# Attention and two MLPs on one core: last rows' scores from block-diagonal queries, the low parts of the first MLP's input made per chunk on VectorE, and a new order

## The chip, the cores and the metric

The kernel runs on one core of a Trainium2 chip. TensorE (PE in the profile) multiplies matrices, VectorE (DVE), ScalarE (ACT) and GpSimd (POOL) do the work between, and SyncE (SP) issues the transfers; each engine takes its own instructions in order. PEld are the loads of the matmuls' stationary operands. The metric is the device time of one launch in microseconds (us).

## The reference, cut to what matters

```python
def _attn_ref(q, k, v, tau):                      # 4 x 8 heads, 576 rows, 64 wide
    scores = (1.0 / np.sqrt(q.shape[-1])) * np.matmul(q, k.transpose(0, 1, 3, 2))
    thresh = np.max(scores, axis=-1, keepdims=True) - tau
    scores = np.where(scores >= thresh, scores, -1000000000.0)
    attn = np.exp(scores - np.max(scores, axis=-1, keepdims=True))
    attn = attn / (np.sum(attn, axis=-1, keepdims=True) + 1e-09)
    return np.matmul(attn, v)
...
x = attn_out, heads side by side                  # 2304 tokens x 512
h = x @ w_in                                      # 512 -> 2048
x = (h * np.tanh(softplus(h))) @ w_out            # first MLP, 2048 -> 512
g = x @ w_gate                                    # 512 -> 1536
x = (g * sigmoid(g) * (x @ w_val)) @ w_out2       # second MLP, 1536 -> 512
```

The weights of the MLPs come as 64-bit words and are turned into floats on the chip.

## The kernel before, in words

**Precision.** A 32-bit factor is split into a high part (the value cast to fp32r, a 32-bit format of TensorE) and a low part (the value less its high part). A product is three matmuls: high with high, high with low, low with high.

**Attention.** Two heads form a pair, and the 16 pairs run one after the other, overlapped. For pairs after the first, `load` brings q and k (128 partitions: 64 dimensions of each head), POOL scales q (L216), ACT casts the high part (L219), POOL makes the low part (L222), and `stack` copies the pieces by 12 transfers into `stk`, where the 128 partitions hold the high part of one head above its low part, so that one matmul covers two of the products. A head has 576 rows: four blocks of 128 and a rest of 64. So a pair has nine score tiles `s`: eight full ones (four matmuls each, 576 columns in two pieces of 320 and 256, each twice), and tile 8, which holds the last 64 rows of both heads. Tile 8 is made by `scores` at L89 with ten matmuls, from columns where the two heads' last rows stand side by side: first all 128 rows against the second head's keys, then the first 64 rows again against the first head's keys. Per tile, DVE takes the row maximum (`rowmax`, L108), POOL adds the threshold (`thresh`, L112), ACT takes the exponential (L118), DVE masks and sums (`mask`, L126). PE transposes the masked rows (L149), ACT copies them to `pt` (L155 to L162), and `av` (L172, 20 matmuls for each of two halves) multiplies by the values. Three score tiles fit in PSUM at once (`s=3`), so a tile waits for the mask of the one three before it.

**First MLP.** Tokens are taken in chunks of 512, the last has 256. For a group of columns of `w_in`, each chunk has a unit per column block: `project` (L533, 12 matmuls, here called a U), the activation on ACT (L565), a high part `gh` on ACT (L550), a low part `gl` on DVE (L553), and `down` (L544, 12 matmuls, here called a D). The chunks' inputs are split too: `x_hi` on ACT (L557) and `x_lo` (L560), the latter on POOL for the chunks after the first, as soon as attention has ended. Chunk 0's parts `x0h` and `x0l` are made during attention. Weights are turned into floats by DVE steps (L445 to L466, `cg` and `cn`), one integer addition on POOL (L452), a cast on ACT (L471) and a low part on DVE (L476); four tiles named `early` are done during attention.

**Order.** All operations of a stage are entered in a planner (`Plan`) with an engine, a cost, what they come after, what slots they take and free, and a rank. For attention the ranks alone fix each engine's order (tables `RANK`, `EARLY`, `XEARLY`); for the MLPs the planner takes, of the operations that are ready, the one with the lowest rank (`MRANK`).

Of the kernel before, what the change touches and what calls it, by code (L numbers as in the profile page):

```python
# [9 lines left out]
F32 = mybir.dt.float32  # L10
# [6 lines left out]
P = 128  # L17
# [27 lines left out]
def attention(tc, cst, q, k, v, x, beside=None, S=576):  # L45
# [18 lines left out]
    ps = ctx.enter_context(tc.tile_pool(name="a_ps", bufs=2, space=PSUM))  # L64

    def load(p, nm, h=None):
        src = dict(q=q, k=k, v=v)[nm][p]
        if nm == "v":
            t = pw.tile([P, 10, 64], F32, tag="vn", name=f"vn{p}", bufs=SLOTS["vn"])
        elif h is None:  # L70
            t = pl.tile([P, S], F32, tag="n", name=f"{nm}n{p}", bufs=SLOTS["n"])
        else:
            if nm + "n" not in st[p]:
                st[p][nm + "n"] = pw.tile([P, 1152], F32, tag="pp", name=f"{nm}d{p}", bufs=SLOTS["pp"])
            for r in (0, 64):
                nc.sync.dma_start(out=st[p][nm + "n"][r:r + 64, S * h:S * h + S], in_=src[64 * h:64 * h + 64, :])
            return
        nc.sync.dma_start(out=t, in_=src)
        st[p][nm + "n"] = t


    def scores(p, i):
# [129 lines left out]
    def inputs(p, nm, what, eng=None):  # L212
# [4 lines left out]
        elif what == "hi":  # L217
            d[nm + "h"] = pl.tile([P, S], F32R, tag="hh", name=f"{nm}h{p}", bufs=SLOTS["hl"])
            nc.scalar.copy(out=d[nm + "h"], in_=src)  # L219
        elif what == "lo":  # L220
            d[nm + "l"] = pl.tile([P, S], F32R, tag="ll", name=f"{nm}l{p}", bufs=SLOTS["hl"])
            eng.tensor_tensor(out=d[nm + "l"], in0=src, in1=f(d[nm + "h"]), op=ALU.subtract)  # L222

    def stack(p, nm, h):
# [4 lines left out]
        for w, a, b in ((0, hi, lo),) if nm == "q" else ((1, hi, lo), (2, lo, hi)):  # L229
            for r, t in ((0, a), (64, b)):  # L230
                nc.sync.dma_start(out=f(d["stk"][r:r + 64, w, 576 * h:576 * h + 576]), in_=f(t[64 * h:64 * h + 64, :]))
# [24 lines left out]
    for p in range(NP):  # L256
# [20 lines left out]
        else:  # L277
            for nm in "qk":
# [136 lines left out]
PERIOD = 17.4
# [382 lines left out]
```

## Time and profile before

| | us |
|---|---|
| median of three runs | 1149.66 (1149.41 to 1150.66) |
| the profiled execution | 1150.61 |
| its span | 1148.8 |
| PE busy | 1115.2, 97% |
| DVE busy | 753.7, 66% |
| ACT busy | 456.3, 40% |
| POOL busy | 246.7, 21% |

The busy shares are means over three stages: the start (to about 29 us), the attention (to about 295 us) and the two MLPs. An engine that shows 66% over the span can be close to full in one stage and nearly idle in another, so the stages are read apart. An entry in brackets behind a row of the timeline is the time for which the engine stood idle before the instruction and what released it. The views used are the busy times by stretches, the chain of work that ended last, the timeline of an engine, the waits, and the groups of instructions by line.

### The profile page before, as it was taken

To read this page: it belongs to the slowest core of one execution; us is meant where nothing else is said; L and a number is where in the kernel's file an instruction comes from. 1 tells how busy PE (TensorE), PEld (TensorE's weight loads), DVE (VectorE), ACT (ScalarE), POOL (GpSimd) and SP (SyncE) were. 2 spreads that over 40 slices of the span, in tenths; PEclk is the share of its full clock that TensorE was granted. 3 is DMA by queue.
4 is the path that set the end of the run, shared out by engine and by line. 5 is a ranking of instruction groups with operands and counts; after the bars stand their busy time and mean duration, and the time that the engine had idled before them with its cause. 6 is when DMAs were issued, how large, how long until landed. Compare 5 with 4: busy or idle time off the path is not lost.

```text
span 1148.8 us, 16265 instructions
## 1 busy us (share of the span) xinstructions
PE 1115.2 (97%) x6088; PEld 925.8 (81%) x6088; DVE 753.7 (66%) x1375; ACT 456.3 (40%) x897; POOL 246.7 (21%) x368
## 2 busy tenths in 40 slices
PE   3999999999799999999999999999999999999998
PEld 3877877777578888888888888888888888888887
DVE  7888888888799672675733699446235952694333
ACT  4888878887535222322322344223112211222111
POOL 3444455453843010110100121102000200120000
PEclk9999999999999999999999999999999999999999
DMA  6666566563123120120110122111001210120012
GB/s 181 171 179 155 154 166 159 158 160 96 37 74 94 37 73 1 38 74 13 61 37 1 37 74 74 37 34 59 19 0 38 75 54 1 37 74 1 1 74 92
DMA packets 34271, 83.24 MB, mean 72 GB/s; under 512 B 5264, under 2 KB 5264, under 8 KB 34192
## 3 DMA queue, kind: packets, MB, share of 16 engines
q1 hardware_dynamic: 34192, 82.20, 24.9%
q8 instruction: 48, 0.79, 0.3%
q14 instruction: 31, 0.25, 0.1%
HBM read 50.92 MB, written 4.72 MB: 48 GB/s over the span
## 4 chain that ended last, share of the span: by engine, by line
PE 90%; DVE 5%; POOL 2%; issue 1%; ACT 1%; DMA 1%; SPq 0%; DVEq 0%; POOLq 0%; ACTq 0%
PE h L533 28%; PE y L544 16%; PE v L533 13%; PE y L546 12%; PE s L89 7%; PE av L172 6%; PE tg L149 6%; PE rg L197 1%; DVE cg L462 1%; POOL xlo L560 1%; DVE gl L553 1%; POOL cg L452 1%; DVE cg L458 0%; DVE cn L466 0%; DMA qn<-in_dram 0%
## 5 line engine op out<-in xcount | busy, mean ns | idle before, releaser
L452 POOL TENSOR_TENSOR cg<-cg,ione 128x512 int32<-128x512 int32 x68 | 92.3, 1361 | 630.8 <-DVE cg L448 630.8
L550 ACT CAST gh<-s 128x512 fp32r<-128x512 f32 (+1 forms) x140 | 80.9, 579 | 255.6 <-DVE s L574 129.4
L533 PE MATMUL h<-xhi,wt 128*128 128x512 f32 (+1 forms) x576 | 170.4, 362 | 0.0
L553 DVE TENSOR_TENSOR gl<-s,gh 128x512 fp32r<-128x512 f32 (+1 forms) x140 | 99.2, 710 | 108.1 <-ACT gh L550 106.7
L574 DVE TENSOR_TENSOR s<-v,u 128x512 f32<-128x512 f32 (+1 forms) x60 | 38.1, 634 | 171.8 <-PE v L533 171.8
L89 PE MATMUL s<-stk 128*128 128x320 f32 (+5 forms) x672 | 126.0, 316 | 18.3 <-DVE stk L246 15.4
L126 DVE SCALAR_TENSOR_TENSOR pp<-s,sm,e 128x576 f32<-128x576 f32 x144 | 115.6, 810 | 11.6 <-ACT e L118 9.6
L533 PEld LDWEIGHTS h<-xhi,wt 128*128 128x128 f32 x576 | 104.7, 189 | 17.4
L89 PEld LDWEIGHTS s<-stk 128*128 128x128 f32 (+1 forms) x672 | 97.7, 189 | 26.0 <-issue 14.4
L108 DVE TENSOR_REDUCE sm<-s 128x1 f32<-128x576 f32 x144 | 105.7, 754 | 16.2 <-PE s L89 16.0
L544 PE MATMUL y<-gh,wt 128*128 128x512 f32 (+1 forms) x400 | 113.3, 368 | 0.0
L118 ACT ACTIVATE e<-s,sm 128x576 f32<-128x576 f32 x144 | 103.2, 753 | 7.8 <-DVE sm L108 7.2
L533 PE MATMUL h<-xlo,wt 128*128 128x512 f32 (+1 forms) x288 | 104.5, 363 | 0.0
L149 PE MATMUL tg<-idf,pp 128*128 128x128 f32 x656 | 102.0, 280 | 0.3
L155 ACT COPY pt<-tg 128x384 f32<-128x384 f32 x192 | 88.5, 489 | 32.8 <-PE tg L149 32.5
L533 PE MATMUL h<-xhi,early 128*128 128x512 f32 (+1 forms) x320 | 95.1, 364 | 1.1 <-ACT s L565 1.1
L565 ACT ACTIVATE s<-h 128x512 f32<-128x512 f32 (+1 forms) x80 | 44.2, 556 | 126.8 <-PE h L533 121.7
L571 ACT ACTIVATE u<-h 128x512 f32<-128x512 f32 (+1 forms) x60 | 33.3, 555 | 148.5 <-PE h L533 148.5
L149 PEld LDWEIGHTS tg<-idf,pp 128*128 128x128 f32 x656 | 73.6, 142 | 14.8 <-ACT qh L219 4.9
L172 PE MATMUL av<-pt,vn 128*64 128x256 f32 (+1 forms) x640 | 84.7, 411 | 0.0
L544 PEld LDWEIGHTS y<-gh,wt 128*128 128x128 f32 x400 | 72.5, 189 | 12.6
L583 DVE TENSOR_TENSOR acc<-y,acc 128x512 f32<-128x512 f32 (+1 forms) x100 | 60.6, 635 | 30.4 <-PE y L544 30.4
(110 smaller groups left out, 2165.4 us busy)
## 6 DMA issues: line engine op xcount, KB each, us to landing
raw<-in_dram SPq DMA_DIRECT2D x64, 512.0 KB, 3.6
stk<-kh SPq DMA_DIRECT2D x60, 144.0 KB, 3.3
stk<-kl SPq DMA_DIRECT2D x60, 144.0 KB, 3.4
vn<-in_dram SPq DMA_DIRECT2D x16, 320.0 KB, 2.8
out_dram<-acc SPq DMA_DIRECT2D x18, 256.0 KB, 2.0
qn<-in_dram SPq DMA_DIRECT2D x15, 288.0 KB, 3.2
kn<-in_dram SPq DMA_DIRECT2D x15, 288.0 KB, 3.6
stk<-qh SPq DMA_DIRECT2D x30, 144.0 KB, 3.9
```

The costliest lines, as they stand in the source:

```text
L89: nc.tensor.matmul(out=s[out, c0:c0 + n], lhsT=stk[:, 0, qc:qc + out.stop - out.start], rhs=stk[:, w, kc:kc + n], start=w == 1, stop=w == 2)
L108: nc.vector.tensor_reduce(out=d["nm"][:, i:i + 1], in_=d["s", i], op=ALU.max, axis=AX.X, negate=True)
L118: nc.scalar.activation(out=e, in_=d["s", i], func=AF.Exp, bias=d["nm"][:, i:i + 1])
L126: nc.vector.scalar_tensor_tensor(out=d["pp", c][:, 576 * h:576 * h + 576], in0=d["s", i], scalar=d["th"][:, i:i + 1], in1=d["e", i], op0=A ...
L149: nc.tensor.transpose(g[:, 128 * m:128 * m + 128], d["pp", c][:, o:o + 128], idf)
L155: nc.scalar.copy(out=t[:, m0:m0 + n, 128 * (c % 2):128 * (c % 2) + 128], in_=g[:, 0:n])
L172: nc.tensor.matmul(out=d["av", u][64 * h:64 * h + 64, 0:n], lhsT=d["vn"][:, 5 * h + j], rhs=d["pt", u][:, 5 * h + j if j < 4 else 4, 0:n], ...
L452: nc.gpsimd.tensor_tensor(out=g, in0=g, in1=self.ione.to_broadcast([P, 512]), op=ALU.add)
L533: nc.tensor.matmul(out=un[nm], lhsT=w[:, a, P * d:P * d + P], rhs=parts(x, d, un["c0"], un["n"]), start=d == 0 and k == 0, stop=d == ND - ...
L544: nc.tensor.matmul(out=y[:, 0:un["n"]], lhsT=w[:, a, P * d:P * d + P], rhs=x, start=first and k == 0, stop=last and k == 2)
L546: nc.tensor.matmul(out=y, lhsT=x[:, P * d:P * d + P], rhs=w[:, a], start=first and k == 0, stop=last and k == 2)
L553: V.tensor_tensor(out=un["gl"], in0=un["s"], in1=f(un["gh"]), op=ALU.subtract)
```

## The change

Four things are changed.

1. Tile 8 of pairs 1 to 15 is made from two tiles `qt`, set to zero once, whose left upper and right lower 64x64 blocks receive the last 64 query columns of the two heads: four copies of 64x64 on POOL (`tails`). The keys are no longer taken from `stk` but from the high and low parts of k as loaded, with both heads' keys in the same order of columns; for that k is stored 640 columns wide, with the last 64 in front of and behind the others. Six matmuls take the place of ten. The high and low parts of q and k get slots of their own (`q=2, k=2`).
2. In the first MLP `x_lo` runs on DVE, and a chunk's `x_hi` and `x_lo` come after the first U step of the chunk before it.
3. The numbers that set the order are all new (ranks, `EARLY`, `XEARLY`, `MRANK`, and some slots of weights).
4. The host stores k in the new layout.

```diff
+    qt = [pl.tile([P, 2, P], F32R, name=f"qt{i}") for i in range(2)]
+    for t in qt:
+        nc.vector.memset(f(t), 0.0)
...
+    def mine(nm, h):
+        return slice(64, 640) if nm == "k" and h == 0 else slice(0, 576)
...
+        elif p:
+            for c0, n in ((0, 320), (320, 256)):
+                for w, (a, b) in enumerate(((0, "h"), (0, "l"), (1, "h"))):
+                    nc.tensor.matmul(out=s[:, c0:c0 + n], lhsT=d["qt"][:, a], rhs=d["k" + b][:, 64 + c0:64 + c0 + n], start=w == 0, stop=w == 2)
         else:
...
-            d[nm + "h"] = pl.tile([P, S], F32R, tag="hh", name=f"{nm}h{p}", bufs=SLOTS["hl"])
+            d[nm + "h"] = pl.tile([P, src.shape[1]], F32R, tag=nm + "h", name=f"{nm}h{p}", bufs=SLOTS[nm])
...
+    def tails(p):
+        d = st[p]
+        d["qt"] = qt[p % 2]
+        for w, t in enumerate((d["qh"], d["ql"])):
+            for h in range(2):
+                a = slice(64 * h, 64 * h + 64)
+                nc.gpsimd.tensor_scalar(out=d["qt"][a, w, a], in0=f(t[a, 512 - 512 * h:576 - 512 * h]), scalar1=1.0, scalar2=1.0, op0=ALU.mult, op1=ALU.mult)
...
+            op("Pool", .8, tails, key=("t",), after=[("q", "stack", 1)], take=["qt"], free=["q"])
...
-SLOTS = dict(wraw=3, wc=6, sm=4, wt=4, s=3, g=2, e=4, pp=3, pt=2, rw=6, rs=6, vn=1, stk=2, n=1, hl=2)
-
-PERIOD = 17.4
+KW = 640
+SLOTS = dict(wraw=3, wc=4, sm=4, wt=4, s=3, g=2, e=4, pp=3, pt=2, rw=5, rs=4, q=2, k=2, qt=2, vn=1, stk=2, n=1)
+
+PERIOD = 16.77
...
-    def x_lo(d, c0, n, eng):
-        eng.tensor_tensor(out=parts(1, d, c0, n), in0=acc1[:, d, c0:c0 + n], in1=f(parts(0, d, c0, n)), op=ALU.subtract)
+    def x_lo(d, c0, n):
+        V.tensor_tensor(out=parts(1, d, c0, n), in0=acc1[:, d, c0:c0 + n], in1=f(parts(0, d, c0, n)), op=ALU.subtract)
...
-            plan.op("ACT", aS(n), lambda a=(d, c0, n): x_hi(*a), ("x", c0, d), [], [], [], r)
-            plan.op("Pool", po(n), lambda a=(d, c0, n): x_lo(*a, nc.gpsimd), ("X", c0, d), [("x", c0, d)], [], [], r)
+
+            ready = [("U", units1[0]["G"] * (ci - 1), 0)]
+            plan.op("ACT", aS(n), lambda a=(d, c0, n): x_hi(*a), ("x", c0, d), ready, [], [], r)
+            plan.op("DVE", dv(n), lambda a=(d, c0, n): x_lo(*a), ("X", c0, d), [("x", c0, d)], [], [], r)
...
-    out = [pairs(inputs["q"]), pairs(inputs["k"]), blocks(inputs["v"]), inputs["tau"].reshape(1)]
+    out = [pairs(inputs["q"]), heads(inputs["k"], np.r_[M:S, 0:S]), blocks(inputs["v"]), inputs["tau"].reshape(1)]
```

PE, tile 8 of the last pair, before: behind the second half of the `av` product and three transposes stand the ten matmuls of `s_8`, then the broadcast `rg` of the row sums and the next transposes.

```order
L172 MATMUL av_1_3982<-pt_1_3810,vn_3788 64x320 x10
L149 MATMUL tg_1_6_4011<-idf,pp_1_3919 128x128 x3
L89 MATMUL s_8_4018<-stk_3595 128x320 x2
L89 MATMUL s_8_4018<-stk_3595 128x192 x2
L89 MATMUL s_8_4018<-stk_3595 128x64 x2
L89 MATMUL s_8_4018<-stk_3595 64x320 x2
L89 MATMUL s_8_4018<-stk_3595 64x256 x2
L197 MATMUL rg_0_4031<-idf,rw_0_4008 128x128 x2
```

PE, the same place after.

```order
L183 MATMUL av_1_3986<-pt_1_3809,vn_3794 64x320 x10
L160 MATMUL tg_1_6_4013<-idf,pp_1_3919 128x128 x3
L106 MATMUL s_8_4022<-kh_3637,qt_97 128x320
L106 MATMUL s_8_4022<-kl_3674,qt_97 128x320
L106 MATMUL s_8_4022<-kh_3637,qt_97 128x320
L106 MATMUL s_8_4022<-kh_3637,qt_97 128x256
L106 MATMUL s_8_4022<-kl_3674,qt_97 128x256
L106 MATMUL s_8_4022<-kh_3637,qt_97 128x256
L208 MATMUL rg_0_4032<-idf,rw_0_4017 128x128 x2
```

The block's neighbours on PE are the same ones; its 2304 columns have become 1728.

POOL, one pair inside the attention, before: the low part of k (`kl`), thresholds (`sm` with `tau`), the scaling of the next q (`qn`), the sum's addition (`sm` alone) and the low part of q (`ql`).

```order
L222 TENSOR_TENSOR kl_3173<-kn_3073,kh_3136 128x576
L112 TENSOR_SCALAR sm_3091<-sm_3091,tau 128x1 x2
L216 TENSOR_SCALAR qn_3197<-qn_3197,tau 128x576
L112 TENSOR_SCALAR sm_3091<-sm_3091,tau 128x1
L177 TENSOR_SCALAR sm_3091<-sm_3091 128x4
```

POOL, the same place (of a later pair) after.

```order
L233 TENSOR_TENSOR kl_3425<-kn_3317,kh_3387 128x640
L123 TENSOR_SCALAR sm_3351<-sm_3351,tau 128x1 x2
L188 TENSOR_SCALAR sm_3351<-sm_3351 128x4
L251 TENSOR_SCALAR qt_97<-qh_3034 64x64 x2
L251 TENSOR_SCALAR qt_97<-ql_3060 64x64 x2
L227 TENSOR_SCALAR qn_3449<-qn_3449,tau 128x576
L123 TENSOR_SCALAR sm_3351<-sm_3351,tau 128x1 x3
```

The sum's addition has moved ahead of the scaling, the four copies stand between them, and three thresholds come behind the scaling where one did.

DVE, the first steps of the first MLP, before (the steps of four weight tiles, and the first low parts `gl` of the activations behind them; the low parts `xlo` were on POOL, five of them ahead of the next integer addition `cg`).

```order
L455 TENSOR_SCALAR cn<-raw 128x512
L445 TENSOR_SCALAR cg<-raw 128x512
L448 SCALAR_TENSOR_TENSOR cg<-raw,cg 128x512
L455 TENSOR_SCALAR cn<-raw 128x512
L458 TENSOR_SCALAR cg<-cg 128x512
L462 SCALAR_TENSOR_TENSOR cg<-raw,cg 128x512
L458 TENSOR_SCALAR cg<-cg 128x512
L466 SCALAR_TENSOR_TENSOR cn<-cn,cg 128x512
L462 SCALAR_TENSOR_TENSOR cg<-raw,cg 128x512
L553 TENSOR_TENSOR gl<-s,gh 128x512
```

DVE, from the last step of attention (`acc`) after.

```order
L221 TENSOR_TENSOR acc<-av_1_4111,rs_1_4122 128x320
L582 TENSOR_TENSOR xlo<-acc,xhi 128x512 x4
L575 TENSOR_TENSOR gl<-s,gh 128x512
L467 TENSOR_SCALAR cg<-raw 128x512
L470 SCALAR_TENSOR_TENSOR cg<-raw,cg 128x512
L477 TENSOR_SCALAR cn<-raw 128x512
L467 TENSOR_SCALAR cg<-raw 128x512
L470 SCALAR_TENSOR_TENSOR cg<-raw,cg 128x512
L480 TENSOR_SCALAR cg<-cg 128x512
L582 TENSOR_TENSOR xlo<-acc,xhi 128x512
L484 SCALAR_TENSOR_TENSOR cg<-raw,cg 128x512
L480 TENSOR_SCALAR cg<-cg 128x512
```

The first `gl` has moved ahead of the weight steps, and the `xlo` have come to DVE in fours. On POOL the first MLP then has only the integer additions left.

## Rows read from the trace of the kernel before

**Rows 1.** Busy times by stretches: length, then engines' busy us (and counts), granted clock, DMA.

```profile
29.00:278.90 249.90, 247.87 (x1929) 199.23 (x1929) 219.38 (x476) 203.70 (x437) 119.11 (x258) 1.00 0.60 159
...
294.69:344.69 50.00, 42.42 (x174) 33.98 (x175) 46.65 (x57) 24.81 (x46) 32.95 (x23) 0.93 0.21 64
```

**Rows 2.** The chain of work that ended last: start us, us, what.

```profile
59.68 2.84 PE av L172 x20
...
76.52 2.84 PE av L172 x20
...
366.90 2.72 PE y L544 x12
```

**Rows 3.** Timeline of PE in one pair: start us, us, engine, line, operation, count.

```profile
62.75 1.45 PE L89 MATMUL s<-stk 128*128 128x320 f32 x10
...
64.04 0.38 PE L197 MATMUL rg<-idf,rw 128*128 128x128 f32 x2
...
64.51 0.78 PE L89 MATMUL s<-stk 128*128 128x320 f32 x4
...
65.12 0.82 PE L149 MATMUL tg<-idf,pp 128*128 128x128 f32 x6
...
65.92 0.43 PE L89 MATMUL s<-stk 128*128 128x320 f32 x2
...
66.07 0.40 PE L89 MATMUL s<-stk 128*128 128x256 f32 x2
...
66.18 0.28 PE L89 MATMUL s<-stk 128*128 128x256 f32 x1
```

**Rows 4.** Timeline of POOL and DVE around the same pair.

```profile
58.66 0.74 POOL L216 TENSOR_SCALAR qn<-qn,tau 128x576 f32<-128x576 f32 x1 [1.71 <-DMA qn<-in_dram]
...
69.40 0.31 POOL L191 TENSOR_SCALAR rw<-fold,sm 128x64 f32<-128x64 f32 x1
...
60.64 0.81 DVE L126 SCALAR_TENSOR_TENSOR pp<-s,sm,e 128x576 f32<-128x576 f32 x1
```

**Rows 5.** The waits: engine, line, waited for: us in total, times, longest us.

```profile
PE s L89 <- DVE stk L246: 15.4, 3, 14.1
...
PE s L89 <- DVE pp L126: 2.7, 2, 1.9
```

**Rows 6.** Timeline of POOL in the start.

```profile
27.13 0.74 POOL L216 TENSOR_SCALAR qn<-qn,tau 128x576 f32<-128x576 f32 x1 [3.13 <-DMA qn<-in_dram]
```

**Rows 7.** Timeline of DVE, POOL, PE and ACT at the first MLP's start.

```profile
295.19 0.69 DVE L448 SCALAR_TENSOR_TENSOR cg<-raw,cg 128x512 int32<-128x512 int32 x1
...
295.80 1.53 DVE L455 TENSOR_SCALAR cn<-raw 128x512 int32<-128x512 int32 x1
...
311.76 1.75 DVE L553 TENSOR_TENSOR gl<-s,gh 128x512 fp32r<-128x512 f32 x1
...
295.41 7.65 POOL L560 TENSOR_TENSOR xlo<-acc,xhi 128x512 fp32r<-128x512 f32 x5 [1.89 <-ACT xhi L557]
...
305.02 9.63 POOL L560 TENSOR_TENSOR xlo<-acc,xhi 128x512 fp32r<-128x512 f32 x6
...
304.26 0.50 PE L533 MATMUL h<-xhi,early 128*128 128x512 f32 x1 [1.10 <-ACT s L565]
...
313.56 0.50 PE L544 MATMUL y<-gl,early 128*128 128x512 f32 x1 [4.46 <-DVE gl L553]
...
314.77 1.05 PE L544 MATMUL y<-gh,early 128*128 128x512 f32 x2
...
316.05 1.05 PE L544 MATMUL y<-gh,early 128*128 128x512 f32 x2
...
338.13 1.14 PE L544 MATMUL y<-gh,early 128*128 128x512 f32 x2 [2.02 <-ACT acc L581]
...
336.97 0.62 ACT L471 CAST wt<-cn 128x512 fp32r<-128x512 f32 x1 [5.74 <-DVE cn L466]
```

**Rows 8.** Groups by line and shape: count, busy us, mean ns, idle before.

```profile
L560 DVE TENSOR_TENSOR xlo<-acc,xhi 128x512 fp32r<-128x512 f32 x12 | 8.7, 755 | 0.0
```

More of the change, by code (lines that the diff above doesn't have):

```diff
@@ L70, in load @@
         elif h is None:
-            t = pl.tile([P, S], F32, tag="n", name=f"{nm}n{p}", bufs=SLOTS["n"])
+            t = pl.tile([P, KW], F32, tag="n", name=f"{nm}n{p}", bufs=SLOTS["n"])[:, 0:src.shape[1]]
         else:
@@ L75, in load @@
             for r in (0, 64):
-                nc.sync.dma_start(out=st[p][nm + "n"][r:r + 64, S * h:S * h + S], in_=src[64 * h:64 * h + 64, :])
+                nc.sync.dma_start(out=st[p][nm + "n"][r:r + 64, S * h:S * h + S], in_=src[64 * h:64 * h + 64, mine(nm, h)])
             return
@@ L230, in stack @@
             for r, t in ((0, a), (64, b)):
-                nc.sync.dma_start(out=f(d["stk"][r:r + 64, w, 576 * h:576 * h + 576]), in_=f(t[64 * h:64 * h + 64, :]))
+                nc.sync.dma_start(out=f(d["stk"][r:r + 64, w, 576 * h:576 * h + 576]), in_=f(t[64 * h:64 * h + 64, mine(nm, h)]))
+    def tails(p):
[5 more added lines that the diff above has]
+                nc.gpsimd.tensor_scalar(out=d["qt"][a, w, a], in0=f(t[a, 512 - 512 * h:576 - 512 * h]), scalar1=1.0, scalar2=1.0, op0=ALU.mult, op1=ALU.mult)
     def first(p, what, nm, h, w=0, eng=None):
@@ L281, in attention @@
                     op("Pool", 1.0, inputs, "q", "scale", nc.gpsimd, key=("q", "scale"), after=[("q", "load")])
-                op("ACT", .573, inputs, nm, "hi", key=(nm, "hi"), after=[("q", "scale") if nm == "q" else ("k", "load")], take=["hl"])
-                op("Pool", 1.4, inputs, nm, "lo", nc.gpsimd, key=(nm, "lo"), after=[(nm, "hi")], free=["n"])
+                op("ACT", .573 + .053 * (nm == "k"), inputs, nm, "hi", key=(nm, "hi"), after=[("q", "scale") if nm == "q" else ("k", "load")], take=[nm])
+                op("Pool", 1.4 + .15 * (nm == "k"), inputs, nm, "lo", nc.gpsimd, key=(nm, "lo"), after=[(nm, "hi")], free=["n"])
+            op("Pool", .8, tails, key=("t",), after=[("q", "stack", 1)], take=["qt"], free=["q"])
             op("DMA", .82, load, "v", key=("v", "load"), take=["vn"])
@@ L286, in attention @@
                 for h in range(2):
-                    op("DMA", cost, stack, nm, h, key=(nm, "stack", h), after=[(nm, "lo"), ("q", "stack", 0)][:2 if (nm, h) != ("q", 0) else 1], take=["stk"] * ((nm, h) == ("q", 0)), free=["hl"] * h)
+                    op("DMA", cost, stack, nm, h, key=(nm, "stack", h), after=[(nm, "lo"), ("q", "stack", 0)][:2 if (nm, h) != ("q", 0) else 1], take=["stk"] * ((nm, h) == ("q", 0)), )
         for i in range(9):
             c, h = divmod(i, 2)
-            op("PE", .53 if i < 8 else 1.2, scores, i, key=("S", i), after=[(y, "stack", z) for y in "qk" for z in ([h] if i < 8 else [0, 1])], take=["s"], free=["stk"] if i == 8 else [])
+            op("PE", .53 if i < 8 else .81 if p else 1.2, scores, i, key=("S", i), after=[(y, "stack", z) for y in "qk" for z in ([h] if i < 8 else [0, 1])] + [("t",)] * (i == 8 and p > 0), take=["s"], free=(["stk"] + ["k", "qt"] * (p > 0)) if i == 8 else [])
             op("DVE", .68, rowmax, i, key=("R", i), after=[("S", i)] + [("R", 0)] * (i > 0), take=["sm"] * (i == 0))
@@ L415 @@
[L415 to L416 removed]
+EARLY = ((-737.77, -380.48, -238.06, -180.98, 74.1, -72.68, -20.2, 117.09, 193.81, 291.92), (86.05, 91.29, 101.59, 166.87, 225.06, 187.35, 303.36, 320.2, 321.27, 335.48), (108.81, 96.97, 157.55, 207.23, 114.16, 239.82, 252.14, 268.7, 331.34, 646.84), (137.49, 176.12, 185.08, 252.81, 342.42, 288.19, 334.09, 348.19, 635.78, 714.97),)
@@ L672, in moes @@
                     plan.op("ACT", aS(n), lambda a=(d, c0, un["n"]): x_hi(*a), ("x2", c0, d), [key], [], [], r + MRANK["x2"])
-                    plan.op("DVE", dv(n), lambda a=(d, c0, un["n"]): x_lo(*a, V), ("X2", c0, d), [("x2", c0, d)], [], [], r + MRANK["x2"])
+                    plan.op("DVE", dv(n), lambda a=(d, c0, un["n"]): x_lo(*a), ("X2", c0, d), [("x2", c0, d)], [], [], r + MRANK["x2"])
             else:
@@ L687 @@
 MSLOTS = dict(h=3, y=5, t=3, g=3, wraw=2, wc=2, wt=11)
-MRANK = dict(X=319.9, wl=-583.5, wa=-1264, wb=369.6, wu=-2583.3, wc=593, wd=428.5, we=18.7, wx=272.7, wh=2429.7, w=589.2, U=-76.1, U2=-833.8, D=-58.3, E=1768.7, V=-350.2, H=-1017.8, O=572.6, S=-939.1, x2=686.6, out=-1641.3)
+MRANK = dict(X=734.9, wl=-450.5, wa=-2390.7, wb=-328.9, wu=-3529.5, wc=990.2, wd=-261.6, we=76, wx=-205.3, wh=5020.7, w=985.1, U=-65.9, U2=-2367.5, D=-48.5, E=2243.8, V=-1039.2, H=-1493.1, O=982.9, S=-1478.8, x2=1088.1, out=-2042.9)
 @with_exitstack
@@ L749, in _layout, with heads @@
     turn = np.r_[M:S, 0:M]
+    def heads(a, order):
+        return a.reshape(-1, 2, S, 64)[:, :, order].transpose(0, 1, 3, 2).reshape(-1, 128, len(order))
     def pairs(a):
```

7 lines of the change are left out of this document (3 added, 4 removed).

## The prediction

> **What bounds the kernel now.** I read the busy times by stretches first, since the page's shares mix three stages. In the attention PE is busy 247.87 of 249.90 us and DVE 219.38 [rows 1]. A busy PE need not be at its peak, so the next view is the chain of work that ended last: in the attention and in the MLPs it is PE nearly throughout. Two neighbouring second halves of the av product start at 59.68 and 76.52 [rows 2], so a pair costs 16.84 us, and what leaves PE's list there can shorten the run. In the MLPs twelve matmuls of 512 columns take 2.72 us [rows 2], 0.227 each, without holes, with one exception: the first 50 us of the first MLP. There PE is busy 42.42 of 50 us, DVE 46.65 and POOL 32.95, and the granted clock is 0.93 of the full 2.4 GHz [rows 1]. So I expect change in three places and nowhere else: at tile 8 in fifteen pairs, at the first MLP's beginning, and in the start of the kernel. In the second half of the first MLP and in the second MLP the queues of PE, DVE and ACT stand in the order in which they stood.
>
> **Tile 8.** The old block runs from 62.75 to 64.04, where rg begins: 1.29 us [rows 3]. The new block is a full tile's four matmuls plus one more of 320 columns and one of 256. A full tile in the same position, behind three transposes, runs from 64.51 to 65.12, 0.61 us; a matmul of 320 columns holds PE from 65.92 to 66.07, 0.15, one of 256 from 66.07 to 66.18, 0.11 to 0.12 [rows 3]. Sum 0.87 us, saving 0.42 per pair, times 15: **6.3 us**. Whether it arrives depends on who feeds PE. The four copies of 64x64 are new on POOL. None is in the trace; the nearest is a copy of 128x64 at 0.31 us [rows 4], so the four cost about 1.25. They stand ahead of the scaling of q, where POOL idles 1.71 us for q's transfer [rows 4]: hidden, as long as the sum's addition, now ahead of them, does not come late. Queued behind the scaling are three thresholds; DVE's mask of tile 5, which starts at 60.64 [rows 4], waits for the first, and with it tile 8's place in PSUM. That mask ends about 1.3 us before tile 8 starts at 62.75, and this is the second cover. The low part of k is 640 columns instead of 576 wide: a ninth more of some 1.4 us on POOL, behind the same thresholds. DVE's mask of tile 6 now stands behind the av result of the pair before; it frees the place for the next pair's tile 0, which PE wants 0.42 us earlier, so some of this may turn into small waits. For such waits I set the lower end at 4, a third lost, and the upper at 8, since PE's small holes within a pair can shrink too in the new order. I take 6.3.
>
> **The first MLP's beginning.** Here the low parts of x are POOL's: 5 in 7.65 us, then 6 in 9.63 [rows 7]. While they run, every DVE step is slow. One of 0.69 us is the last at its usual speed; the next, a plain bit operation, takes 1.53, and a gl later 1.75 [rows 7]. DVE keeps exactly POOL's pace, one step to each of POOL's. As the weight steps stand ahead of gl, the first gl comes so late that PE waits 4.46 us for it; before that it waits 1.10 for the activation, because ACT first casts all 16 high parts, and later 2.02 for ACT, which itself waited 5.74 for a DVE step [rows 7]. That is 7.6 us. After the two long waits matmuls run at 1.2 GHz: from 314.77 to 316.05 three of them pass, 0.427 each [rows 7], 0.20 more than in the rest; there are about nine behind either wait, so 18 x 0.20 = 3.6. Together **11.2 us** that PE loses here.
>
> The change takes the POOL work away and puts the first gl ahead of the weight steps. What is late next? The tightest need is the low parts of the third chunk: PE reaches them after five runs of twelve matmuls, 5 x 2.72 = 13.6 us after the MLP's first matmul, and the last of the four two us later. By then DVE has to do, in its new order, eight xlo, one gl, and nine weight steps. An xlo on DVE is 0.755 [rows 8]; the weight steps I take at 0.43 to 0.69. That is 6.0 + 0.7 + 5 = 11.7, plus about 1.6 before the first high part is cast and about 1.5 of waiting for the first gh: some 14.9, against 15.7. So it fits with little to spare, and later chunks have the 10.9 us of four runs each for four xlo. ACT casts four high parts instead of sixteen ahead of the first activation, so the 1.10 go too. Lower end of the gain 7 (a wait of 3 us stays), upper 11.7; I take **10.7**.
>
> By the Trainium skill (SBUF — State Buffer, "Who interferes with whom") a VectorE instruction with two inputs in SBUF and a GpSimd instruction that reads SBUF lock each other out for a whole instruction. The rows at the MLP's beginning agree, 1.53 and 1.75 us for steps of some 0.4 and 0.7. The same rule speaks against the change as well, since an xlo on VectorE has two such inputs and GpSimd keeps the integer additions; by it the first of the rivals below would come true.
>
> **The start.** PE's first matmul waits 14.1 us for DVE's low part of k; after it PE waits another 1.3 for DVE's low parts and 2.7 for masks [rows 5]. The masks wait for POOL's thresholds, which stand behind the scaling of the second pair's q, for which POOL waits 3.13 us [rows 6]. Now q is loaded ahead of k, and the weight steps that stood between the low parts of k are behind them. The transfers carry the same bytes. Two zero fills come to DVE while it waits for tau, so they cost nothing; without that cover, about half a us. Bounds: -0.5 and 3 (what the two kinds of wait after the first matmul come to, less one). I take half of the upper one, **1.5 us**.
>
> **The sum.** 6.3 + 10.7 + 1.5 = 18.5. The profiled execution took 1150.61 (span 1148.8 and 1.8 around it); less 18.5 it is 1132.1. It lies 0.95 above the median of the three runs, so in the median **1131**. Own range 1127 to 1135.
>
> **Rivals.**
>
> *DVE and POOL still in each other's way (1136).* POOL's integer additions stay, and an xlo or gl that meets one loses about 1.06 us (1.75 less 0.69). Four additions fall into the first 15 us or just behind: 4.2 us of DVE, of which 0.8 is spare, so PE waits 3.4 and then runs nine matmuls at 1.2 GHz, 1.8: 5.2 lost where I left 0.5. That is 1131 + 4.7, about 1136. For it: the pace of DVE beside POOL; against it: four single additions, not a row of eleven.
>
> *The pair's period is not PE's (1137).* If DVE's 2 us of idle time per pair (16.84 less 219.38 spread over the 14.84 pairs in that stretch, 14.8) are all forced by latencies, nothing of the 0.42 arrives: 1131 + 6.3. It decides if those gaps do not shrink when PE comes earlier. Most of DVE's gaps end with PE, which speaks against it.
>
> *No gain at the MLP's beginning (1142).* The change would not do there what it says if the high parts, which now wait for a U step of the chunk before, came too late. They need only the first three of 24 matmuls, so I hold this unlikely.
>
> *Slower: the copies on POOL (1158).* The four copies hold up the thresholds in every pair. Their cover is 1.71 + 1.3 = 3.0 us. To eat the whole gain they have to be late by a further 18.5 / 15 = 1.23 per pair, so the point is 4.25 us for four, 1.06 each. At 1.5 each, 6.0 in all, the loss is 15 x 3.0 = 45 less 18.5, 26 us more than now, 1176; at 1.2 each, 4.8, it is 27 - 18.5 = 8.5 more, 1158. The price of 0.31 for a copy of the same width speaks against it. I take 1158 for it.
>
> **How the numbers follow.** Chances: the forecast 0.69, DVE against POOL 0.14, the period 0.09, no gain at the MLP 0.03, a mixture that ends within 0.2% of before 0.01, slower by the copies 0.04. The range reaches from the forecast's lower end, 1127, to 1138, which takes in the first two rivals and leaves the last three and the forecast's and these rivals' tails, about 2 in 10, outside. 0.2% (2.3 us) is about what a measurement of this kernel can tell from no change. Faster by more: 0.69 + 0.14 + 0.09 + 0.03 = 0.95; within: 0.01; slower: 0.04.
>
> **What the profile after would show.** Tile 8: six matmuls in about 0.87 us, and av products 16.4 us apart; if they stay 16.8 apart with a new wait on DVE or POOL in front of PE, the second rival holds. The MLP's beginning: DVE steps of 0.4 to 0.75 us, no POOL row but the additions, PE's waits of 4.46 and 2.02 gone and the granted clock at 1.00; a PE wait on DVE about 14 us behind the MLP's first matmul is the first rival. The start: PE's first matmul before 14 us and av products of the first pair about 1.5 us earlier. I would be wrong if a POOL copy took over 0.8 us, or if new waits stood elsewhere in the MLPs, where I changed nothing.

## The result, and the profile after

| | before | after |
|---|---|---|
| median, us | 1149.66 (5 runs, 1148.65 to 1151.18) | 1136.82 (5 runs, 1135.03 to 1138.60) |
| the profiled execution, us | 1150.61 | 1138.60 |
| its span, us | 1148.8 | 1136.5 |

The ratio is 0.9886 (95%: 0.9871 to 0.9900). The kernel became 12.8 us faster, where 18.5 was forecast (1131). The time lies in the range 1127 to 1138 and outside the forecast's own 1127 to 1135. The profiled execution is the slowest of the five.

Busy times by stretches (length, then busy us and counts of PE, PEld, DVE, ACT, POOL, granted clock, DMA share, GB/s), after: the attention, the first 50 us of the first MLP, and the 30 us behind them.

```profile
29.00:275.00 246.00, 241.57 (x1862) 193.71 (x1861) 216.93 (x475) 203.10 (x433) 131.55 (x314) 0.99 0.61 161
290.96:340.96 50.00, 50.00 (x230) 41.48 (x231) 45.49 (x80) 29.42 (x56) 13.05 (x9) 1.00 0.24 74
340.96:370.96 30.00, 27.97 (x131) 22.71 (x130) 27.21 (x46) 11.91 (x24) 7.69 (x5) 1.00 0.33 106
```

Before, the 30 us behind the first 50 us of the first MLP:

```profile
344.69:374.69 30.00, 30.00 (x151) 25.54 (x150) 27.73 (x48) 14.78 (x31) 9.17 (x6) 1.00 0.33 102
```

Against [rows 1], the first 50 us of the MLP have no hole left (PE 50.00 instead of 42.42, clock 1.00 instead of 0.93). But PE is idle for 2 us in the next 30, where the kernel before had none, and the attention, which stood at clock 1.00, stands at 0.99. What PE waits for, in the whole execution (us in total, times, longest):

```profile
PE s L96 <- DVE stk L266: 15.4, 2, 13.5
PE s L96 <- DVE pp L137: 3.4, 4, 1.5
PE tg L160 <- ACT pt L166: 2.4, 1, 2.4
PE y L566 <- ACT acc L603: 1.2, 1, 1.2
PE h L555 <- DVE acc L221: 0.7, 1, 0.7
...
PE y L566 <- DVE gl L575: 0.5, 1, 0.5
PE y L568 <- DVE gl L575: 0.3, 1, 0.3
PE y L566 <- DVE acc L605: 0.3, 1, 0.3
```

The waits of 4.46, 2.02 and 1.10 of [rows 7] are gone. New are one of 2.4 for ACT in the attention and three of 1.2, 0.5 and 0.3 in the first MLP. The 0.3 in line L568 is no new one: the kernel before has it too (it is shown further below).

**Tile 8.** The timeline of PE and of POOL in one pair:

```profile
64.74 0.55 PE L160 MATMUL tg<-idf,pp 128*128 128x128 f32 x3
65.05 0.39 PE L106 MATMUL s<-kh,qt 128*128 128x320 f32 x1
...
65.80 0.28 PE L106 MATMUL s<-kh,qt 128*128 128x256 f32 x1
65.92 0.38 PE L208 MATMUL rg<-idf,rw 128*128 128x128 f32 x2
...
76.65 0.54 POOL L251 TENSOR_SCALAR qt<-qh 64x64 fp32r<-64x64 f32 x2
77.25 0.54 POOL L251 TENSOR_SCALAR qt<-ql 64x64 fp32r<-64x64 f32 x2
77.90 0.74 POOL L227 TENSOR_SCALAR qn<-qn,tau 128x576 f32<-128x576 f32 x1
```

The six matmuls run from 65.05 to 65.92, 0.87 us, as summed from [rows 3]. The four copies take 77.90 - 76.65 = 1.25 us, as estimated from [rows 4]. But the scaling behind them no longer waits for q (1.71 us before): the first part of their cover, the idle time that was to hide them, is gone.

**The stages apart.** The table is made from starts of rows in the timelines of PE: the second half of the first pair's av product; from there to the first matmul of the MLPs; from that to the start of the last matmul. The last two columns are k of the third pair, from issue to landing, and the time from the first to the second half of that av product. The kernels are those of the experiments below.

| kernel | first pair's av | to the MLPs | MLPs | k lands after | first to second half |
|---|---|---|---|---|---|
| before | 42.77 | 251.92 | 849.68 | 3.1 | 9.73 |
| before, again | 43.06 | 251.82 | 848.09 | 3.0 | 9.72 |
| after | 45.48 | 245.48 | 841.44 | 7.6 | 13.53 |
| after, again | 43.34 | 246.46 | 841.21 | 6.2 | 11.07 |
| e1, load behind k | 42.03 | 245.88 | 841.33 | 4.1 | 9.72 |
| e2, old tile 8 | 42.18 | 251.49 | 841.22 | 4.9 | 9.72 |
| e3, low parts on POOL | 42.62 | 245.59 | 850.52 | 4.0 | 9.72 |
| e4, new MLP alone | 44.16 | 251.66 | 841.01 | 3.2 | 9.72 |
| e5, small additions | 42.24 | 245.46 | 837.35 | 5.3 | 10.12 |
| e6, copies twice | 42.34 | 247.98 | 841.03 | 5.1 | 9.93 |
| e7, both edits | 41.96 | 245.59 | 837.34 | 4.0 | 9.72 |
| e8, new attention alone | 42.67 | 247.24 | 848.81 | 4.8 | 9.72 |
| e9, planner's number | 43.54 | 247.21 | 837.36 | 6.5 | 11.29 |
| b1, both edits again | 42.65 | 246.44 | 837.37 | 3.8 | 9.73 |

The time from the second half of one pair's av product to that of the next is called the period. The expectations speak of PE's loss in the MLPs: the sum of what its matmuls start further apart than 0.227 us (0.120 for 256 columns), 13.10 us before and 4.86 after.

In the profiled execution of after, the pairs gain 251.92 - 245.48 = 6.4, the MLPs 8.2, and the start loses 2.7.

### The profile page after: what moved, and what is told of

Same layout as the page of the kernel before. It is cut to its first block, busy times and chain, and to the rows that moved or that the text cites. A ratio compares the mean times of both kernels' runs of the same rounds, so it can differ in the third digit from the quotient of the medians.

```text
span 1136.5 us, 16142 instructions
## 1 busy us (share of the span) xinstructions
PE 1105.7 (97%) x6028; PEld 917.5 (81%) x6028; DVE 747.2 (66%) x1393; ACT 457.4 (40%) x897; POOL 240.4 (21%) x412
## 4 chain that ended last, share of the span: by engine, by line
PE 66%; DVE 6%; POOL 1%; ACT 0%; issue 0%; DMA 0%; DVEq 0%
PE h L555 27%; PE y L566 15%; PE v L555 13%; PE y L568 12%; DVE cg L484 1%; DVE gl L575 1%; DVE cg L470 1%; DVE cg L467 1%; DVE cn L488 1%; POOL cg L474 1%; DVE cn L477 1%; DVE xlo L582 1%; DVE cg L480 1%; DVE wt L498 0%; DMA raw<-in_dram 0%
## 5 line engine op out<-in xcount | busy, mean ns | idle before, releaser
L575 DVE TENSOR_TENSOR gl<-s,gh 128x512 fp32r<-128x512 f32 (+1 forms) x140 | 96.5, 691 | 107.7 <-ACT gh L572 106.5
L96 PE MATMUL s<-stk 128*128 128x256 f32 (+2 forms) x522 | 102.8, 320 | 18.8 <-DVE stk L266 15.4
L96 PEld LDWEIGHTS s<-stk 128*128 128x128 f32 x522 | 78.8, 193 | 26.0 <-DVE stk L266 15.8
L605 DVE TENSOR_TENSOR acc<-y,acc 128x512 f32<-128x512 f32 (+1 forms) x100 | 60.6, 634 | 30.4 <-PE y L566 30.4
```

The source lines that it names most:

```text
L96: nc.tensor.matmul(out=s[out, c0:c0 + n], lhsT=stk[:, 0, qc:qc + out.stop - out.start], rhs=stk[:, w, kc:kc + n], start=w == 1, stop=w == 2)
L575: V.tensor_tensor(out=un["gl"], in0=un["s"], in1=f(un["gh"]), op=ALU.subtract)
```

## Experiments

Each compares with runs of the kernel before on the same chip; the changed kernel's ratio to such runs was 0.9886 (the result) and 0.9879 (c1).

**Late k: a load moved.** In the profiled execution the third weight load stands ahead of k, and k lands after 7.6 us. The timelines of the transfers' queue, ACT, PE and DVE (in brackets the idle time before the row, and what ended it):

```profile
28.99 0.45 SPq L463 DMA_DIRECT2D wraw<-in_dram  x1
29.89 0.33 SPq L85 DMA_DIRECT2D kn<-in_dram  x1
...
37.48 0.72 ACT L230 CAST kh<-kn 128x640 fp32r<-128x640 f32 x1 [3.48 <-DMA kn<-in_dram]
...
38.64 0.66 PE L160 MATMUL tg<-idf,pp 128*128 128x128 f32 x4 [2.40 <-ACT pt L166]
...
39.71 0.82 DVE L137 SCALAR_TENSOR_TENSOR pp<-s,sm,e 128x576 f32<-128x576 f32 x1 [2.46 <-ACT e L129]
```

Busy times there (columns as above):

```profile
38.00:42.00 4.00, 3.16 (x19) 2.99 (x20) 2.19 (x4) 3.69 (x11) 2.06 (x3) 0.75 0.27 77
42.00:46.00 4.00, 4.00 (x28) 3.69 (x28) 3.01 (x8) 3.15 (x7) 2.75 (x8) 0.82 0.90 224
```

ACT's cast of k's high part stands ahead of two evacuations (copies of `tg` from PSUM to `pt`) and an exponential; PE waits for the copies, DVE for the exponential, and behind the wait PE runs part of 8 us at 1.2 GHz. E1 moves the load:

```diff
-(108.81, 96.97, 157.55, ...      # EARLY, third tile: rank of the load first
+(115.3, 96.97, 157.55, ...
```

> The changed kernel with one transfer moved: the third weight load (512 KB) is issued behind the four pieces of q for stk instead of ahead of k of the third pair; every other queue keeps its order. Theory (transfers in a queue): k of that pair landed 7.6 us after its issue because the weight load stood ahead of it. Now it lands after 3 to 4.5 us, ACT's wait of 3.48 us for it and PE's wait of 2.40 us behind that go, the granted clock stays at 1.00 from 38 to 46 us, the second half of the first pair's av product starts near 41.7 instead of 45.48, and the median falls from 1136.8 to about 1133. Rival (too many bytes at once, whatever their order): k lands after 6 us or more, and the median stays within 1 us of 1136.8. Rival (the load is now late for DVE): DVE waits for the weight load where its first step on it stands, and what is gained for k is lost there; 1136 or more.

Measured: 1135.48 us, ratio 0.9879 (0.9863 to 0.9896). k lands after 4.1 us, the waits and the low clock are gone (e1, ACT's timeline):

```profile
34.41 0.73 ACT L230 CAST kh<-kn 128x640 fp32r<-128x640 f32 x1
```

E1's busy times:

```profile
38.00:42.00 4.00, 4.00 (x31) 3.53 (x31) 3.49 (x9) 3.43 (x8) 2.31 (x9) 1.00 0.68 174
```

The trace does what the theory said, the median does not (1133 expected). E2 and e3, with the load still ahead, saw k land after 4.9 and 4.0 us: so the order alone does not make it late. Hence the changed kernel once more:

> The changed kernel as it is, to see what of its profiled execution belongs to the kernel. Theory (the late k of the third pair is that execution's own): with the same order, two other kernels saw k land after 4.0 and 4.9 us; so here it lands after 4 to 5 us, ACT waits under 1 us for it, PE not at all, and the profiled time is 1135 to 1136; the median 1135.5 to 1137. Rival (the order makes it, and the others escaped by chance or by their other changes): ACT waits over 2 us again, profiled time about 1138.

Measured: 1135.73 us, ratio 0.9879 (0.9864 to 0.9894); profiled 1137.08, again its slowest. k landed after 6.2 us, ACT waited 2.12 for it, PE 1.0 for ACT. The theory fails: k is late again, and ACT waits over 2 us, as the rival says. But the rival does not hold for all kernels with this order either: in eight executions with the load ahead k landed after 4.0, 4.8, 4.9, 5.1, 5.3, 6.2, 6.5 and 7.6 us, in three with it behind after 3.8, 4.0 and 4.1. The table shows what it costs: nothing up to 4.9, then about as much as it is later (0.2 at 5.1, 0.4 at 5.3, 1.35 at 6.2, 1.6 at 6.5), and 3.8 at 7.6, since the clock falls too. What makes the landing scatter stays open. By the medians of e9 and b1 below it is too rare, or too small, to be measured.

The same cast waits a second time, near 200 us, for the k of the thirteenth pair, whether the load is moved or not (c1, ACT's and PE's timelines):

```profile
201.81 0.73 ACT L230 CAST kh<-kn 128x640 fp32r<-128x640 f32 x1 [1.60 <-issue]
...
202.97 0.66 PE L160 MATMUL tg<-idf,pp 128*128 128x128 f32 x4 [0.52 <-ACT pt L166]
```

That k was issued at 197.66 and landed after 4.1 us, just ahead of the cast. In c1, e8, e9 and b1 it landed after 3.8 to 4.5 us, ACT was idle for 1.34 to 2.03, and the period there is 17.05 to 17.73 us; where it landed after 3.0 to 3.2 (after, e1, e5 and e7) the period is 16.48 or 16.49. In the three traces with the old attention (before, c2 and e4) no cast of k waits longer than 0.3 us. So the new order leaves this cast little slack behind k's landing at two places, and the second makes most of the spread of the column "to the MLPs" between kernels with the new tile 8.

**Tile 8 undone.**

```diff
-        elif p:
+        elif p < 0:
```

> The changed kernel with the ten matmuls of old for tile 8 in all pairs; the four copies on POOL, the wide k and the order stay. Theory (PE sets the pair's period): 15 x 0.42 = 6.3 us come back, periods of 16.84 us, median about 1143. Rival (the new order alone made the period shorter, PE's columns are not the bound): periods stay at 16.4 to 16.5, median 1137 to 1138.5.

Measured: 1141.60 us, ratio 0.9932 (0.9917 to 0.9947). All periods but the last are 16.83 us, as before, in the new order; with six matmuls they are 16.42, but for two that are longer (16.55 and 16.49 in the trace of after). Two neighbouring second halves of the av product in e2, then in after:

```profile
176.84 2.91 PE L183 MATMUL av<-pt,vn 128*64 128x320 f32 x20
...
193.68 2.91 PE L183 MATMUL av<-pt,vn 128*64 128x320 f32 x20
```

```profile
176.97 2.91 PE L183 MATMUL av<-pt,vn 128*64 128x320 f32 x20
...
193.39 2.91 PE L183 MATMUL av<-pt,vn 128*64 128x320 f32 x20
```

Against the changed kernel's two ratios that is 0.46% and 0.53%, 5.3 and 6.1 us, for tile 8 alone: PE's columns set the period.

**The low parts on POOL again.**

```diff
-            plan.op("DVE", dv(n), lambda a=(d, c0, n): x_lo(*a), ...
+            plan.op("Pool", po(n), lambda a=(d, c0, n): x_lo(*a, nc.gpsimd), ...
```

> The changed kernel with the low parts of x on POOL again; ranks and the new dependence of the high parts stay. Theory (POOL's two-input steps slow DVE): at the first MLP's beginning DVE's steps of 0.4 to 0.7 us take 1.5 us and more while POOL has low parts, PE waits again, 8 to 10 us come back, median 1145 to 1147. Rival (the gain is the order's: the first gl ahead of the weight steps, high parts spread out): DVE's steps are slow as before but nobody waits for them, median within 2 us of 1136.8.

Measured: 1145.48 us, ratio 0.9967 (0.9954 to 0.9980), MLPs 850.52. Timeline of POOL, DVE, ACT and PE:

```profile
299.36 6.01 POOL L582 TENSOR_TENSOR xlo<-acc,xhi 128x512 fp32r<-128x512 f32 x4
...
301.03 1.78 DVE L484 SCALAR_TENSOR_TENSOR cg<-raw,cg 128x512 int32<-128x512 int32 x1
302.73 1.50 DVE L480 TENSOR_SCALAR cg<-cg 128x512 int32<-128x512 int32 x1
...
319.80 0.62 ACT L493 CAST wt<-cn 128x512 fp32r<-128x512 f32 x1 [7.36 <-DVE cn L488]
...
320.96 1.22 PE L566 MATMUL y<-gh,early 128*128 128x512 f32 x2 [7.28 <-ACT acc L603]
```

Beside POOL's low parts DVE's steps take 1.5 and 1.8 us again, a weight is late, ACT's cast waits for it, and PE's place in PSUM waits behind that cast. So the new order without the move gains nothing in the MLPs. Whether the move would gain as much in the old order was not run.

**Each half alone.** E4 is the kernel before with the MLP's change, e8 the changed kernel with the MLP as before.

```diff
# e4, to the kernel before
-            plan.op("ACT", aS(n), lambda a=(d, c0, n): x_hi(*a), ("x", c0, d), [], [], [], r)
-            plan.op("Pool", po(n), lambda a=(d, c0, n): x_lo(*a, nc.gpsimd), ...
+            ready = [("U", units1[0]["G"] * (ci - 1), 0)]
+            plan.op("ACT", aS(n), lambda a=(d, c0, n): x_hi(*a), ("x", c0, d), ready, [], [], r)
+            plan.op("DVE", dv(n), lambda a=(d, c0, n): x_lo(*a, V), ...
...
+MRANK = dict(X=734.9, wl=-450.5, ...
# e8, to the changed kernel: the reverse
```

> The kernel before with the change of the first MLP alone (low parts on DVE, the new dependence, the new MLP ranks); the attention is as before. Theory (the parts add up): PE loses 4.9 us in the MLPs as in the changed kernel, where the kernel before loses 13.1; median 1149.7 less 8.2, about 1141.5, and the stalls of 1.2, 0.5 and 0.3 us some 55 to 75 us behind the first MLP's beginning are there too. Rival (they do not: the new attention order hands the early weights over in a better state, or the stalls come from it): gain under 6 us or over 10, stalls elsewhere.

> The changed kernel with the first MLP as before (low parts on POOL, no new dependence, old MLP ranks). Theory (the parts add up): periods of 16.42, PE's loss in the MLPs 13.1 as in the kernel before, so 6.3 and 0.7 to 1.5 are gained, and up to 1.4 lost to k's late landing: median about 1142 to 1143. Rival (the gains overlap, since the MLP's beginning is limited by weights that attention prepares, and an attention that ends sooner hands over less): MLP loss over 15, median 1145 or more.

Measured: e4 1143.14 us, ratio 0.9946 (0.9931 to 0.9961); e8 1143.66, 0.9942 (0.9928 to 0.9957). They gain 0.54% and 0.58%, together 1.12%; the changed kernel gains 1.14% and 1.21%. The parts add up. E4's MLPs take 841.01 us, with stalls of 1.0, 0.5 and 0.3 at the same places, so these come with the MLP's own order. E4's median is 1.6 us above the expectation. In its trace the first pair is 1.1 to 1.4 us later than in the two traces of the kernel before, with the same order there; why stays open, and that it explains the median is not shown.

**What stalls the MLP.** Where PE waits 1.2 us, the timeline of POOL, DVE, ACT and PE after:

```profile
341.44 1.42 POOL L474 TENSOR_TENSOR cg<-cg,ione 128x512 int32<-128x512 int32 x1 [2.24 <-DVE cg L470]
...
341.88 1.26 DVE L477 TENSOR_SCALAR cn<-raw 128x512 int32<-128x512 int32 x1
...
345.33 0.68 DVE L488 SCALAR_TENSOR_TENSOR cn<-cn,cg 128x512 f32<-128x512 f32 x1
...
346.05 0.62 ACT L493 CAST early<-cn 128x512 fp32r<-128x512 f32 x1 [1.34 <-DVE cn L488]
...
347.06 1.55 ACT L603 COPY acc<-y 128x512 f32<-128x512 f32 x3
...
347.69 0.50 PE L566 MATMUL y<-gh,early 128*128 128x256 f32 x2 [1.23 <-ACT acc L603]
```

A DVE step that takes 0.42 us alone takes 1.26 beside POOL's addition. Ten steps were held up so between 291 and 361, by 0.75 to 0.85 us each. The weight that DVE finishes at 346 is needed much later, but its cast stands in ACT's queue ahead of the copy that frees PE's place in PSUM. The second wait, for a low part `gl` of DVE, comes the same way: ACT casts the high part for it behind a weight for which ACT has waited 1.32 us (ACT's and PE's timelines).

```profile
352.76 0.62 ACT L493 CAST early<-cn 128x512 fp32r<-128x512 f32 x1 [1.32 <-DVE cn L488]
...
354.45 0.50 PE L566 MATMUL y<-gl,wt 128*128 128x512 f32 x1 [0.52 <-DVE gl L575]
```

The third, 0.28 us at 366.14, is for DVE's own addition (L605). E5 cuts the additions on POOL to 8 columns:

```diff
-            nc.gpsimd.tensor_tensor(out=g, in0=g, in1=self.ione.to_broadcast([P, 512]), op=ALU.add)
+            n = 8 if low == "DVE" else 512      # g, ione cut to n columns
+            nc.gpsimd.tensor_tensor(out=g, in0=g, in1=self.ione.to_broadcast([P, n]), op=ALU.add)
```

> The changed kernel with POOL's integer additions in the MLPs cut from 512 to 8 columns (the rest of the weights' rounding is left out); no instruction moves. Theory (lock): the DVE steps that take 1.2 to 1.5 us beside an addition take 0.4 to 0.7 again, DVE is no longer full from 301 to 361, and PE's stalls of 1.2, 0.5 and 0.3 us at 346, 354 and 365 go: MLP loss from 4.86 to about 2.5, median about 1134. Rival (the twelve xlo and the weight steps fill DVE by themselves, or ACT's order makes the stalls): the stalls stay within a third of what they were, median within 1 us of the changed kernel's.

Measured: 1131.80 us, ratio 0.9848 (0.9831 to 0.9864), more than expected; MLPs 837.35, 4.1 less than after, and no DVE step is held up in the first 70 us. In the same queue order no wait in the MLPs is left but the first (L556):

```profile
PE s L96 <- DVE stk L266: 15.4, 2, 13.5
PE s L96 <- DVE pp L137: 3.6, 4, 1.6
PE h L556 <- DVE acc L221: 0.7, 1, 0.7
...
```

E7 leaves the addition whole and tells the planner of it (the load is moved as in e1):

```diff
-            ("DVE", .335, c, "c", "a", [], []),
+            ("DVE", 1.185 if low == "DVE" else .335, c, "c", "a", [], []),
```

> The changed kernel with the third weight load behind the pieces of q, and with one number of the MLP's planner changed: the DVE step beside POOL's addition is entered at 1.185 instead of 0.335 us, as the trace shows it (1.27 less the 0.08 by which steps overlap). Theory (the stalls at 346 to 365 come because the order was made for a DVE that the additions do not slow, so ACT's casts of weights stand ahead of what PE needs): the stalls shrink from 2.1 to under 1 us, MLP loss under 3.5, median about 1134. Rival (DVE is full whatever the order): the waits move and stay as long in sum, median 1135 to 1137.

Measured: 1132.04 us, ratio 0.9845 (0.9831 to 0.9860), MLPs 837.34: all 4.1 us, more than expected, without taking the hold-up away: eight DVE steps in the first 70 us still take 0.68 to 0.85 longer, ten in the changed kernel. Busy times of e7 10 to 70 us behind the MLP's first matmul:

```profile
298.00:358.00 60.00, 60.00 (x289) 50.61 (x288) 56.10 (x100) 32.50 (x63) 16.38 (x11) 1.00 0.32 97
```

ACT's timeline of e7:

```profile
337.71 1.95 ACT L603 COPY acc<-y 128x512 f32<-128x512 f32 x3
...
340.11 0.58 ACT L603 COPY acc<-y 128x512 f32<-128x512 f32 x1
341.64 0.62 ACT L493 CAST early<-cn 128x512 fp32r<-128x512 f32 x1 [0.95 <-DVE cn L488]
```

And the same stretch of the changed kernel:

```profile
301.00:361.00 60.00, 58.25 (x277) 48.20 (x276) 56.93 (x101) 30.62 (x63) 17.98 (x12) 1.00 0.30 97
```

DVE is as full as there (56.10 and 56.93 of 60), so a full DVE was not the cause. The casts of weights now stand behind the copies, and ACT's wait of 0.95 for DVE costs PE nothing. E5 shortens the addition itself too, but between 341.88 and 346.01, where DVE ends the weight's step in the trace of after, no DVE row waits for POOL: it was the held-up step that cost the time there. So the stall needs both: a held-up DVE step, and a queue made as if there were none.

E9 has the planner's number without the moved load; b1 is e7 measured again beside it:

> The changed kernel with only the planner's number for the step beside POOL's addition changed (0.335 to 1.185 us), the third weight load ahead of k as in the changed kernel. Theory (the MLP's stalls and the late k are two separate things): MLP loss 0.8 us, and k lands after 4 to 7.6 us, which costs 0 to 3 us by execution: median 1132.0 to 1133.5, scatter wider than with the load behind. Rival (the load's place costs nothing in the median): within 0.5 us of the kernel with both.

> The changed kernel with both edits, the planner's number and the third weight load behind the pieces of q, measured longer on the same chip as the kernel with the number alone. Theory: MLP loss 0.8 us, k lands after 3 to 4.5 us, median about 1132, ratio to the kernel before 0.9845, faster than the changed kernel's 0.988 by more than the interval. Rival (the earlier result was a good draw): ratio 0.9865 or more.

Measured: e9 1131.94 us, ratio 0.9844 (0.9828 to 0.9859), profiled 1134.26 with k after 6.5 us; b1 1132.56, 0.9841 (0.9827 to 0.9856). The planner's number is worth 4 us; the moved load nothing that the median shows. B1 beats both kernels, the one before by 1.6%.

**The cover of the copies.**

```diff
-                nc.gpsimd.tensor_scalar(out=d["qt"][a, w, a], ...
+                for _ in range(2):
+                    nc.gpsimd.tensor_scalar(out=d["qt"][a, w, a], ...
```

> The changed kernel with each of the four 64x64 copies made twice, so that POOL has 1.2 us more per pair ahead of the scaling of q. Theory of the prediction (cover of 3.0 us, of which four copies use 1.25): all of it is hidden, periods stay at 16.42, median within 1 us of the changed kernel's. Rival (the scaling no longer waits for q in the new order, 0.11 us instead of 1.71, so the first part of the cover is gone and the thresholds behind it come late): periods of 16.6 to 17.2, 3 to 12 us more, median 1139 to 1148.

Measured: 1138.06 us, ratio 0.9898 (0.9884 to 0.9913), about 0.2% more than the changed kernel on the same chip (1135.73 in c1), more than the theory and less than the rival. The periods between the fourth and the fifteenth pair are 16.42, but for 17.00, 17.19 and 16.94 in three of them. In those three POOL also has a low part of the first chunk (`x0l`), as in the first of these; in two of them PE is seen to wait behind it:

```profile
193.21 1.28 POOL L756 TENSOR_TENSOR x0l<-acc,x0h 128x512 fp32r<-128x512 f32 x1
...
195.67 0.44 PE L208 MATMUL rg<-idf,rw 128*128 128x128 f32 x2 [0.42 <-POOL rw L200]
```

In a plain pair 1.2 us more are hidden even without the wait for q; where POOL also makes an `x0l`, they are not. So the cover holds, but not everywhere. The period of 17.19 is the one that the late k lengthens too (ACT waits 0.81 there), so not all of it belongs to the copies.

**The start of the kernel before.**

> The kernel before as it is, for a second trace of its start. Theory (the start's term was about right, and executions scatter): in eight traces with the new start the first half of the first pair's av product began between 31.95 and 32.90 us; with the old start it began at 33.04 once and at 34.44 once; here it begins between 33.0 and 34.5, so the start's own gain is between 0.7 and 2.1 us. Rival (the 33.04 stood at the slow end and the start gains nothing): it begins under 32.9. The median within 0.2% of the kernel before.

Measured: 1150.22 us, ratio 0.9999 (0.9990 to 1.0008); the first half of the first pair's av product begins at 33.34, later than all eleven with the new start (31.95 to 32.95). In e4, whose attention is the old one, it begins at 34.44. The new start does gain there, against the middle of the eleven (32.31) by 0.7 and 1.0 us.

## Why the prediction was right and wrong

**Right: the direction, the bound, tile 8.** The sum's term of 6.3 came as 5.3 to 6.1 in the medians (e2), made of 0.87 against 1.29 us per pair. The rival of a period that is not PE's is refuted by e2, where ten matmuls in the new order give 16.83. The copies cost 0.31 each as priced; of their cover of 3.0 us the wait for q (1.71) was not there any more, the rest was enough.

**Wrong in size: the first MLP's beginning, 10.7 forecast.** The mechanism was right: with the low parts off POOL the 11.2 us that PE lost in the first 50 us are gone, and e3 brings 9.1 back, at another wait (7.28 for ACT). The tight point, the third chunk's low parts 13.6 us behind the first matmul, passed without a wait. The step that failed is "what is late next": I checked 15 us, in which DVE had slack, and left half a us for the rest. The next thing late stood 57 us behind the beginning, with smaller ones at 63 and 75. These and one at 597 us make up the 4.1 us by which e5 and e7 are shorter (841.44 against 837.35 and 837.34). The last is not the change's: the kernel before has it at the same place, as long; the loss there is 0.6 us in both. Before, then after:

```profile
900.24 0.50 PE L546 MATMUL y<-wt,gl 128*128 128x512 f32 x1 [0.33 <-DVE gl L553]
```

```profile
888.25 0.50 PE L568 MATMUL y<-wt,gl 128*128 128x512 f32 x1 [0.32 <-DVE gl L575]
```

So the change gave back some 3.5 us. The first rival named the cause, POOL's additions and DVE. It counted four additions where two fell into the first 15 us (at 297.72 and 299.91), priced 1.06 us for a held-up step where up to 0.85 came, and put the wait at the wrong place: the longest was for ACT, whose in-order queue stood behind a weight that DVE finished late. New waits elsewhere in the MLPs were the prediction's own sign of being wrong. They stand in the first half of the first MLP, behind its first 50 us, where the prediction expected no change. Its sentence on the second half of the first MLP and on the second MLP held nearly: by the tiles' names PE's queue is as before from 23 us behind the beginning, ACT's differs up to 62 us and DVE's up to 69, and behind that only in a few places, where no new wait stands. Net 8.2 in the profiled executions; the 11.2 had also been read from an execution at the long end, since a second trace of the kernel before has 848.09 for the MLPs instead of 849.68.

**Wrong: the start, 1.5 forecast.** The first av half does begin earlier, 31.95 to 32.95 in eleven traces against 33.04, 33.34 and 34.44. But the step that gave the term failed: the waits after PE's first matmul, from which its bounds were made, did not shrink. Up to the first av half they come to 4.0, 3.4 and 3.6 us in the three traces with the old start and to 4.2 to 5.5 in the eleven. What came earlier is the first matmul itself, 13.30 to 13.64 against 14.08, 14.43 and 15.83. Left out was also the next stop of the same queue: the weight load now ahead of k. In the middle of the eleven traces the second half begins at 42.62 against 42.77, 43.06 and 44.16, 0.15 and 0.44 earlier than in the two traces of the kernel before; in the profiled execution k's late landing made it a loss of 2.7. Bounds of -0.5 to 3 were too narrow for that.

So of 18.5 us, 5.3 to 6.1 came for 6.3, some 6 to 8 for 10.7 (6.2 in e4's median, 6.9 to 8.2 in the traces), and under 1 for 1.5; the medians of the whole give 12.8 and 13.8. Tile 8 was right because its term was a count of rows on the engine that sets the pace; both others were judged at the place that was edited and not at the next stop of the queues behind it. The forecast's own upper end of 1135 did not follow from its terms, whose lower ends, 4 + 7 - 0.5 = 10.5, give 1139. That the time lies inside 1138 is in part luck: the room up there was made for two rivals, neither of which came as it was told, though the first one's 1136 lies near the measured time.

## What to carry to other kernels

When work moves from one engine to another, follow the in-order queues past the edited place: a step that is late and needed much later still stops everything queued behind it, on an engine (ACT here) to which the change gives no new work. If an order is planned from costs, enter the cost that a step has beside its neighbours, as the trace shows it; one number was worth 4 us here. A cast that stands close behind a transfer's landing is such a step too. Before a term is set against one trace, look at how far the same stretch varies in a second one.

## What the runs showed of the hardware

A DVE step held up by POOL's addition is not always one with two inputs: the prediction's row of 1.53 us is a bit operation of one input, and so is the step at 341.88, which took 1.26 us instead of 0.42, until 0.28 us behind the addition's end. The one that started first kept its time: three low parts `xlo` from 309.17 on took 0.68 to 0.69 us each, and the addition that started at 309.33 took 2.62 instead of 1.04. Steps that read one input from PSUM were not held up: the additions at 658.97 and 659.57 took 0.68 beside POOL's from 659.13 to 660.17, as elsewhere. By the Trainium skill (SBUF — State Buffer, "Who interferes with whom") a VectorE step with at most one SBUF input does not contend, except in its two-port modes, which `tensor_scalar` can enter; the rows agree with both halves of it, though no row shows a step's mode.

The third pair's k, a transfer of 320 KB, landed after 4.0 to 7.6 us in eight executions with the same order, behind a load of 512 KB. In the three traces where that load stood behind it, it took 3.8 to 4.1 us, and the 288 KB of the old layout took 3.0 to 3.2 in three more.
